# One transfer for both batches in the tail stores, and a last output piece halved between two engines

## The chip, the cores and the metric

The kernel runs on one core of a Trainium2 chip. The metric is the device time of one launch in microseconds. Before the change it was 333.6 us, the median of 3 runs (333.51 to 333.68).

## The reference

A sliding-window attention with ALiBi bias feeds a gated feed-forward block:

```python
B, H, S, D = 8, 8, 576, 64
scores = q @ k.transpose(0, 1, 3, 2) / np.sqrt(D) + slopes * -abs(rel)   # where 0 <= rel < 128
attn = softmax(scores)
x = (attn @ v).transpose(0, 2, 1, 3).reshape(B * S, H * D)               # 4608 x 512
g = x @ w_gate                                                           # 512 x 1536
out = (g * sigmoid(g) * (x @ w_val)) @ w_out                             # 4608 x 512, float32
```

## The kernel before, in words

The 4608 tokens are handled in 9 blocks of 512. Blocks 0 to 7 hold the first 512 tokens of one batch each. A batch has 576 tokens, so 64 are left over in each of the 8 batches; block 8, the tail block, collects these 8 times 64 tokens. Its four tiles of 128 rows hold one pair of batches each: rows 0 to 63 of tile `j` are the last 64 tokens of batch `2j`, rows 64 to 127 those of batch `2j + 1`. In the output in memory those two groups of 64 rows lie 576 rows apart.

The output product of a block is a seven-product scheme, the generator `strassen(n, t)`. For `t` = 0 and 1 it makes the tiles `t` (called `top`) and `t + 2` (called `low`), each 128 rows by 512 columns in float32. Each product is 6 matmuls into a 128x256 piece of PSUM (`X`, `Y` or `p2`); VectorE (`half_plus`, L605) or ScalarE (L612, L623, L626) takes the piece out, and `store` (L507) sends finished rows to memory. A `yield` stands after each product.

Block 8 is the last work of the kernel, and its output is written nowhere earlier. Its two generators are advanced in a fixed order; one step of generator 0 is done earlier, and then

```python
for t in (1, 0, 1, 0, 1, 0, 1, 0, 0, 1, 0, 1, 1):
    next(ends[t])
```

By this order the stores of block 8 are, in time: the left half of tile 1 (second product of generator 1), all of tile 0 (sixth product of generator 0), the right half of tile 3 (fifth of generator 1), all of tile 2 (seventh of generator 0), the right half of tile 1 (sixth of generator 1), and the left half of tile 3 (seventh of generator 1). The last piece, `low[:, 0:HC]` of generator 1 with HC = 256 columns, is taken from `X` by one VectorE instruction (L639).

Before the change a store of a tail tile is two issues of 64 rows, one for each batch. The first of these six stores puts both on SyncE's queue (SP); the other five put one on SP's queue and one on ScalarE's (ACT). Stores of blocks 0 to 7 are one issue of 128 rows on SP's queue. SP has no other work at the end, and ACT has no compute left after the piece `u2s` of generator 1.

Of the kernel before, what the change touches and what calls it, by code (L numbers as in the profile page):

```python
# [16 lines left out]
P = 128  # L17
# [39 lines left out]
def kernel(  # L57
# [10 lines left out]
    nc = tc.nc  # L68
    B, H, S, D = q.shape
    NTOK, DM = out.shape  # L70
# [3 lines left out]
    NSUP = B // 2  # L74
# [418 lines left out]
        val(n, m, wide(n, m, "v"), c0)  # L493
        yield

    def rows_of(n, j):
        if n == 8:
            return [(0, 64, 2 * j * S + 512), (64, 128, (2 * j + 1) * S + 512)]
        return [(0, 128, n * S + j * P)]

    held_stores = []
    queue_unit = [None]

    def store(n, j, osb, c0=0, c1=512, two=False):
        def now():
            for i, (p0, p1, r0) in enumerate(rows_of(n, j)):
                (nc.scalar if two and i else nc.sync).dma_start(out[r0:r0 + p1 - p0, c0:c1],  # L507
                                                                osb[p0:p1, c0:c1])
        if queue_unit[0] is None:
            now()  # L510
        else:
            held_stores.append((queue_unit[0], now))

    def project(n, j, pool, tag, bufs):
        po = pool.tile([P, DM], FP32, name="po", tag=tag, bufs=bufs)
        for m0 in range(0, NMB, 4):
            for i in range(m0, m0 + 4):
                m = NMB - 1 - i if n == 0 else i
                nc.tensor.matmul(po, hT[n][:, m, j * P:(j + 1) * P], wo_sb[:, m, :],  # L519
                                 start=(i == 0), stop=(i == NMB - 1))  # L520
            if m0 + 4 == NMB:
                osb = opool.tile([P, DM], FP32, name="osb", tag="osb")
                nc.scalar.mul(osb, po, 0.5)
                store(n, j, osb)
            yield
# [5 lines left out]
    HC = DM // 2  # L531
# [40 lines left out]
    def strassen(n, t):  # L572

        h = hT[n]
        A11, A12 = h[:, 0:HM, 0:256], h[:, HM:NMB, 0:256]
        S1, A22 = h[:, 0:HM, 256:512], h[:, HM:NMB, 256:512]
        S2, S3, S4 = hsum[n]
        cols = slice(t * P, (t + 1) * P)
        end = n == NBLK - 1
        seeded = SEVEN_FROM <= n + 1 < NBLK  # L580
        factor = 1.0 if n >= SEVEN_FROM else 0.5
        if end:
            X, Y = (ps_a.tile([P, HC], FP32, name="po", tag="a", bufs=4) for _ in range(2))
            p2 = ps_f.tile([P, HC], FP32, name="p2", tag="gv")
        else:
            po = ps_f.tile([P, 2, HC], FP32, name="po", tag="po", bufs=1)
            X, Y = po[:, 0, :], po[:, 1, :]
            p2 = (ps_f.tile([P, HC], FP32, name="p2", tag="gv") if seeded
                  else ps_a.tile([P, HC], FP32, name="p2", tag="a"))
        top, low = (opool.tile([P, DM], FP32, name="osb", tag="osb") for _ in range(2))  # L590
        if end and t:
            spare = [opool.tile([P, DM], FP32, name="osb", tag="osb") for _ in range(2)]
            p1s, p5s, u2s = spare[0][:, 0:HC], spare[0][:, HC:DM], spare[1][:, 0:HC]
        else:
            p1s, p5s, u2s = (supool.tile([P, HC], FP32, name=i, tag=i, bufs=1)
                             for i in ("p1s", "p5s", "u2s"))

        def product(dst, a, b, start=False):
            for m in range(HM):
                nc.tensor.matmul(dst, a[:, m, cols], b[:, m, :], start=(start and m == 0),  # L600
                                 stop=(m == HM - 1), skip_group_check=True)

        def half_plus(dst, a, b):
            with tc.high_priority() if n + 1 < SEVEN_FROM else ExitStack():
                nc.vector.scalar_tensor_tensor(out=dst, in0=a, scalar=factor, in1=b,  # L605
                                               op0=ALU.mult, op1=ALU.add)

        product(X, A11, B11, True)
        if seeded:
            nc.scalar.copy(p2, X)  # L610
        else:
            nc.scalar.mul(p1s, X, factor)  # L612
        yield
        product(p2, A12, B21, not seeded)
        if seeded:
            nc.vector.tensor_scalar_mul(top[:, 0:HC], p2, factor)
        else:
            half_plus(top[:, 0:HC], p2, p1s)
        if end and t:
            store(n, t, top, 0, HC)  # L620
        yield
        product(Y, S1, T1, end)
        nc.scalar.mul(p5s, Y, factor)  # L623
        yield
        product(X, S2, T2)
        nc.scalar.mul(u2s, X, factor)  # L626
        yield
        product(X, S3, T3)
        half_plus(low[:, HC:DM], X, p5s)
        if end and t:  # L630
            store(n, t + 2, low, HC, DM, True)
        yield
        product(Y, S4, B22)
        half_plus(top[:, HC:DM], Y, u2s)
        store(n, t, top, HC if end and t else 0, DM, end)
        yield
        product(X, A22, T4)
        if end:
            nc.vector.tensor_scalar_mul(low[:, 0:HC], X, factor)  # L639
        else:  # L640
            nc.scalar.mul(low[:, 0:HC], X, factor)
        store(n, t + 2, low, 0, HC if end and t else DM, end)
        yield


# [123 lines left out]
    def ffn():  # L769

        for n in range(NBLK):
            if n > 1:
                parts = chain(strassen(n - 1, 0), strassen(n - 1, 1))
# [38 lines left out]
            if n > 1:  # L812
                assert next(parts, 0) == 0
        ends = [strassen(NBLK - 1, t) for t in range(2)]
        tail = ExitStack()
        for n, k, name, which in seven_steps():
            if k == 0 and n > SEVEN_FROM:
                assert next(parts, 0) == 0
                parts = chain(strassen(n - 1, 0), strassen(n - 1, 1))
# [291 lines left out]
```

## Time and profile before

| What | Value |
|---|---|
| median of 3 runs | 333.6 us (333.51 to 333.68) |
| the profiled execution: time, span | 334.02 us, 332.2 us |
| TensorE busy | 323.4 us, 97% of the span |
| VectorE, ScalarE, GpSimd busy | 263.8, 224.3, 111.0 us |
| granted TensorE clock | 0.998 |
| stores from SP, 256 KB each | 32 issues, 2.4 us (median) from issue to landing |
| tail stores from SP | 5 of 64 KB and 2 of 128 KB, 2.3 and 2.5 us |
| tail stores from ACT | 3 of 64 KB and 2 of 128 KB, 2.6 us each |

The span runs from the first to the last instruction that the profile shows; the device time of the same execution is 1.8 us longer. "DMA share" in a table of windows is the mean busy share of the core's 16 DMA engines. A packet is one piece of memory that a DMA engine moves; for these stores it is one row, 2 KB for a whole tile and 1 KB for a half. A queue named q1 is SP's, q10 is ACT's.

### The profile page before, as it was taken

The page shows a single profiled execution, that of the slowest core. Times are in us where ns is not written, and L with a number is a line of the kernel's source. Part 1 is how long each engine was busy: PE and PEld are TensorE (multiplying, and loading weights), DVE is VectorE, ACT ScalarE, POOL GpSimd, SP SyncE. Part 2 cuts the span into 40 slices and gives each one's busy share as a digit, 9 for nine tenths or more (in the row PEclk, how much of TensorE's full clock was granted, in tenths as well). Part 3 has the DMA queues.
Part 4 walks back from the last instruction along what each step waited for, and adds up shares of the span by engine and source line. Part 5 has one row for each costly group of instructions (what it writes and reads, how often), then busy time and mean ns, then how long its engine had stood idle before and what let it go on. Part 6 is the DMA issues. An engine that isn't in the chain of part 4 may idle for free.

```text
span 332.2 us, 7692 instructions
## 1 busy us (share of the span) xinstructions
PE 323.4 (97%) x2911; PEld 216.1 (65%) x2911; DVE 263.8 (79%) x643; ACT 224.3 (68%) x446; POOL 111.0 (33%) x138
## 2 busy tenths in 40 slices
PE   8999999999999999999999999999999999999994
PEld 4665465444455656556556555566788888888884
DVE  4678878999796779877999799997754985775683
ACT  4886777464677868687777677774577666776650
POOL 8977776394963244537253100000000000000000
PEclk9999999999999999999999999999999999999999
DMA  9999999999999999999999991412100101001014
GB/s 152 174 180 176 175 186 166 121 145 173 143 179 170 137 185 143 170 142 155 173 161 174 135 180 32 83 32 79 65 32 35 63 2 63 32 36 64 2 63 129
DMA packets 167654, 39.09 MB, mean 118 GB/s; under 512 B 155456, under 2 KB 163264, under 8 KB 167616
## 3 DMA queue, kind: packets, MB, share of 16 engines
q0 software_dynamic: 118880, 18.62, 80.6%
q1 hardware_dynamic: 48048, 19.35, 33.8%
q10 hardware_dynamic: 688, 0.62, 0.6%
q8 instruction: 23, 0.38, 0.5%
q14 instruction: 15, 0.12, 0.1%
HBM read 37.91 MB, written 9.44 MB: 143 GB/s over the span
## 4 chain that ended last, share of the span: by engine, by line
PE 75%; DVE 16%; ACT 4%; issue 3%; DVEq 0%; ACTq 0%
PE po L600 16%; PE pg L452 13%; PE pv L452 13%; PE gX L689 10%; PE gY L689 5%; PE av L392 4%; DVE uu L471 4%; PE p L600 3%; PE ps L322 3%; PE gZ L689 2%; DVE ex L334 2%; DVE x L396 2%; ACT tt L470 1%; PE po L519 1%; ACT exc L364 1%
## 5 line engine op out<-in xcount | busy, mean ns | idle before, releaser
L452 PE MATMUL pv<-xT,wv_sb 128*128 128x512 f16 (+2 forms) x312 | 76.5, 363 | 0.5 <-DVE uu L471 0.4
L452 PE MATMUL pg<-xT,wg_sb 128*128 128x512 f16 (+2 forms) x324 | 76.6, 355 | 0.1
L470 ACT ACTIVATE tt<-pg 128x512 f16<-128x512 f32 x68 | 41.0, 605 | 32.7 <-PE pg L452 31.3
L328 ACT ACTIVATE ex<-ps 128x512 f16<-128x512 f32 x96 | 50.9, 610 | 4.9 <-PE ps L322 4.9
L471 DVE SCALAR_TENSOR_TENSOR uu<-tt,pg 128x512 f16<-128x512 f16 x67 | 45.6, 680 | 10.4 <-ACT tt L470 9.8
L194 POOL DMA_DIRECT2D kn<-in_k_dram x39 | 33.4, 861 | 47.7 <-DMA kT<-kn 40.7
L452 PEld LDWEIGHTS <-wg_sb 128*128 128x128 f16 x324 | 28.8, 98 | 24.5 <-issue 2.2
L452 PEld LDWEIGHTS <-wv_sb 128*128 128x128 f16 x312 | 27.9, 98 | 25.5 <-issue 2.8
L600 PEld LDWEIGHTS <-hT 128*128 128x128 f16 x384 | 37.2, 98 | 10.7 <-issue 0.8
L188 POOL DMA_DIRECT2D va<-in_v_dram x40 | 34.3, 861 | 15.0 <-DMA kn<-in_k_dram 4.0
L194 POOL DMA_DIRECT2D qn<-in_q_dram x39 | 33.4, 864 | 9.2 <-DMA va<-in_v_dram 5.7
L484 ACT CAST hT<-pv 128x512 f16<-128x512 f32 x44 | 26.3, 598 | 12.9 <-PE pv L452 12.9
L600 PEld LDWEIGHTS <-S 128*128 128x128 f16 x288 | 27.5, 98 | 8.2 <-issue 1.9
L334 DVE TENSOR_TENSOR ex<-ex,m_reg 128x1024 f16<-128x1024 f16 x42 | 28.6, 684 | 3.9 <-ACT ex L328 3.8
L396 DVE TENSOR_TENSOR x<-av,rec 128x256 f16<-128x256 f32 x72 | 28.5, 418 | 0.4
L600 PE MATMUL po<-T,S 128*128 128x256 f16 x192 | 25.9, 273 | 0.3 <-ACT u2s L626 0.3
L600 PE MATMUL po<-T,hT 128*128 128x256 f16 x192 | 26.0, 273 | 0.0
L364 ACT ACTIVATE exc<-psc 128x512 f16<-128x512 f32 x40 | 21.4, 608 | 1.4 <-PE psc L360 1.3
L743 DVE TENSOR_TENSOR hT<-s,v 128x512 f16<-128x512 f16 x18 | 7.6, 423 | 17.7 <-ACT s L742 17.7
L392 PEld LDWEIGHTS <-ex 128*128 128x128 f16 x384 | 17.6, 97 | 4.6 <-issue 1.5
L485 DVE TENSOR_TENSOR hT<-uu,hT 128x512 f16<-128x512 f16 x44 | 18.3, 417 | 2.0 <-ACT hT L484 1.0
L392 PE MATMUL av<-va,ex 128*128 128x65 f16 x384 | 19.4, 193 | 0.6 <-ACT ex L328 0.3
(131 smaller groups left out, 550.6 us busy)
## 6 DMA issues: line engine op xcount, KB each, us to landing
out_dram<-osb SPq DMA_DIRECT2D x32, 256.0 KB, 2.4
va<-in_v_dram POOLq DMA_DIRECT2D x32, 128.0 KB, 8.6
qn<-in_q_dram POOLq DMA_DIRECT2D x31, 128.0 KB, 8.3
kn<-in_k_dram POOLq DMA_DIRECT2D x31, 128.0 KB, 8.3
wg_sb<-in_moe_w_gate_dram POOLq DMA_DIRECT2D x6, 256.0 KB, 7.6
wo_sb<-in_moe_w_out_dram POOLq DMA_DIRECT2D x3, 512.0 KB, 8.2
wv_sb<-in_moe_w_val_dram POOLq DMA_DIRECT2D x5, 256.0 KB, 7.6
kn<-in_k_dram POOLq DMA_DIRECT2D x8, 64.0 KB, 10.3
```

What stands on the lines that cost most here:

```text
L188: nc.gpsimd.dma_start(va[rank][p0:p1, :, 0:D], src)
L194: nc.gpsimd.dma_start(t_[p0:p1], src)
L328: nc.scalar.activation(e[:, o:o + 2, :], banks[q4][par], AF.Exp, scale=scale)
L334: nc.vector.tensor_mul(e[:, o, :], e[:, o, :], reg[:, o, :])
L392: nc.tensor.matmul(av[:, j, :], w, val, start=(n == 0), stop=(n == len(todo) - 1))
L396: nc.vector.tensor_mul(x[:, 4 * half:4 * half + 4, :], av[:, :, 0:D], rec.broadcast_to([P, 4, D]))
L452: close.after = nc.tensor.matmul(ps[:, c0:c1], w[:, kb, ms], xT[n][:, kb, c0:c1], start=(kb == 0 and c0 == 0), stop=(kb == NKB - 1 and c1 ...
L470: nc.scalar.activation(tt, pg[:, c0:c1], AF.Tanh, scale=0.5)
L471: nc.vector.scalar_tensor_tensor(out=uu, in0=tt, scalar=one if (n, m) == PIN else 1.0, in1=pg[:, c0:c1], op0=ALU.add, op1=ALU.mult)
L484: nc.scalar.copy(h, pv)
L600: nc.tensor.matmul(dst, a[:, m, cols], b[:, m, :], start=(start and m == 0), stop=(m == HM - 1), skip_group_check=True)
L689: nc.tensor.matmul(dst[:, i, :], w[:, kb, c0 + i * P:c0 + (i + 1) * P], a[:, kb, :], start=(start and i == 0 and kb == 0), stop=(i == 1 an ...
```

## The change

A store of a tail tile becomes one issue: the output in memory is seen as (batch pair, batch of the pair, token, column), and the 128 rows of the tile go to a view of 2 x 64 rows. All of these go to SP's queue but one: the whole store of tile 2 goes to ACT's. The last piece, 128x256, is taken from PSUM by two instructions, columns 0 to 127 on VectorE and 128 to 255 on ScalarE. Stores of blocks 0 to 7 have the same rows, columns and queue as before.

```diff
-    def rows_of(n, j):
-        if n == 8:
-            return [(0, 64, 2 * j * S + 512), (64, 128, (2 * j + 1) * S + 512)]
-        return [(0, 128, n * S + j * P)]
...
+    tails_out = out.rearrange("(j n t) d -> j n t d", j=NSUP, n=2)
+
-    def store(n, j, osb, c0=0, c1=512, two=False):
+    def store(n, j, osb, c0=0, c1=512, by=None):
         def now():
-            for i, (p0, p1, r0) in enumerate(rows_of(n, j)):
-                (nc.scalar if two and i else nc.sync).dma_start(out[r0:r0 + p1 - p0, c0:c1],
-                                                                osb[p0:p1, c0:c1])
+            to = tails_out[j, :, 512:S, c0:c1] if n == 8 else out[n * S + j * P:n * S + (j + 1) * P, c0:c1]
+            (by or nc.sync).dma_start(to, osb[:, c0:c1])
...
         if end and t:
-            store(n, t + 2, low, HC, DM, True)
+            store(n, t + 2, low, HC, DM)
...
-        store(n, t, top, HC if end and t else 0, DM, end)
+        store(n, t, top, HC if end and t else 0, DM)
         yield
         product(X, A22, T4)
-        if end:
+        if end and t:
+            nc.vector.tensor_scalar_mul(low[:, 0:P], X[:, 0:P], factor)
+            nc.scalar.mul(low[:, P:HC], X[:, P:HC], factor)
+        elif end:
             nc.vector.tensor_scalar_mul(low[:, 0:HC], X, factor)
         else:
             nc.scalar.mul(low[:, 0:HC], X, factor)
-        store(n, t + 2, low, 0, HC if end and t else DM, end)
+        store(n, t + 2, low, 0, HC if end and t else DM, nc.scalar if end and not t else None)
```

## The prediction

> **What bounds the kernel now.** I read the page first: TensorE is busy for 97% of the span, so an edit that touches no matmul can only act before TensorE starts or after it ends. The edit touches the stores of the tail block alone, which all lie after 323 us. The chain of waits over the last 6 us says where TensorE lets go:
>
> ```profile
> span 332.2 us, 7692 instructions
> ...
> by line: PE po L600 24.8%; DVE osb L639 5.3%; issue 0.3%
> ...
> 325.98 1.98 PE po L600 x18
> 327.96 0.02 issue
> 327.98 0.42 DVE osb L639
> ```
>
> The last matmul ends at 327.96 and the last piece is out of PSUM at 328.40. The remaining 3.8 us belong to no engine. The windows table says who works there (the last two columns are DMA share and GB/s):
>
> ```profile
> 327.00:327.50 0.50, 0.50 (x7) 0.44 (x6) 0.20 (x2) 0.00 (x0) 0.00 (x0) 1.00 0.91 193
> 327.50:328.00 0.50, 0.44 (x5) 0.15 (x2) 0.34 (x2) 0.00 (x0) 0.00 (x0) 1.00 0.97 307
> ...
> 329.00:329.50 0.50, 0.00 (x0) 0.00 (x0) 0.00 (x0) 0.00 (x0) 0.00 (x0) 1.00 0.97 322
> ...
> 330.00:330.50 0.50, 0.00 (x0) 0.00 (x0) 0.00 (x0) 0.00 (x0) 0.00 (x0) 1.00 0.58 176
> 330.50:331.00 0.50, 0.00 (x0) 0.00 (x0) 0.00 (x0) 0.00 (x0) 0.00 (x0) 0.69 0.00 0
> ```
>
> From 327.0 to 330.4 all 16 DMA engines are near full. So the end is set by the DMA engines emptying the output: the last packets end at about 330.4, and 1.8 us later (completions, then the closing barrier) the span ends. Whatever slows these packets moves the end one for one. The tail stores are issued here (start, length, queue):
>
> ```profile
> 323.41 5.54 SPq L507 DMA_DIRECT2D out_dram<-osb  x7
> ...
> 325.89 3.37 ACTq L507 DMA_DIRECT2D out_dram<-osb  x5
> ...
> 328.44 0.52 SPq L507 DMA_DIRECT2D out_dram<-osb  x1
> ...
> 328.68 0.58 ACTq L507 DMA_DIRECT2D out_dram<-osb  x1
> ```
>
> The unit price of moving rows comes from three DMA views. First one 128-row, 256 KB store alone (318.3 to 320.3), then the whole of ACT's queue (300 to 334), then the first tail store, two times 64 rows of 1 KB (324 to 326):
>
> ```profile
> DMA packets 144, 0.26 MB, mean 131 GB/s; under 512 B 16, under 2 KB 16, under 8 KB 144
> ...
> q1 hardware_dynamic: 144, 0.26, 34.2%
> ```
> ```profile
> q10 hardware_dynamic: 400, 0.46, 4.0%
> ```
> ```profile
> q1 hardware_dynamic: 155, 0.13, 25.0%
> ```
>
> A 128-row store is 128 row packets and 16 tiny ones, so all 16 engines end a share of it. ACT's five 64-row stores make 5 x (64 + 16) = 400 packets: 16 shares again. Price of a 2 KB row: 34.2% x 16 engines x 2.0 us / 128 = 85 ns, 84 ns without the tiny packets. Price of a 1 KB row: 25.0% x 16 x 2.0 / 124 data packets recorded = 64 ns in the 64-row stores. In the last stretch (329.6 to 330.4, where the DMA view gives 46.3% and 34.3% for the two queues, 244 packets, 52 of them tiny) it is 51 ns; half of a 2 KB row would be 42 ns; the commonest single record is 46 ns, which I take.
>
> **The change part by part.**
>
> *Seven issues on SP become five, five on ACT become one.* A 128-row issue takes 0.33 us on SP (the store at 318.35), the 64-row ones 0.47 to 0.58 on SP and 0.56 to 0.78 on ACT. This removes about 2 us of queue time on SP and 2.5 on ACT, beside the transfers and not on the path, except that the last issue no longer stands at 328.68 behind ACT's earlier ones (0.3 us). Worth that much only if the DMA engines are idle then.
>
> *The shape of the transfer.* This is the step that decides. Every transfer in this trace has 64 or 128 as the outermost count on both sides and ends in 16 shares. The new view of memory begins with a count of 2, the batches, 576 rows apart, which can't be folded into the 64 rows; the SBUF side begins with 128. No row shows how such a pair is dealt out. Bounds: 16 shares by rows, as all stores now (8 rows for each engine), or shares by the outermost count that both sides have, that is 2 shares of 64 rows on 2 engines. I take the second: each share must be a whole piece of both patterns, and the only cut at the outermost level that 2 and 128 both allow is in two.
>
> Sum for 2 engines. Both get 64 rows of each of the six stores: four half tiles, 4 x 64 x 46 ns = 11.8 us, and two whole ones, 2 x 64 x 84 ns = 10.8 us; 22.6 us of packets for each engine, where now the same 1 MB is spread over 16. The first store is issued at 323.41; the first packet follows 0.83 us (the store at 318.35) to 1.2 us later, so at about 324.4. The first store alone holds its engines to 327.3, and the second is issued at 325.88, so the two engines never run dry. Last packet: 324.4 + 22.6 = 347.0. With the same 1.8 us behind it the span is 348.8, that is 16.6 us more than 332.2. The profiled execution (334.02, 1.8 beside its span) becomes 350.6; the runs' median lies 0.4 lower, so **350.2 us**.
>
> Bounds of that sum: 42 and 84 ns with the early start give 324.2 + 21.5 + 1.8 = 347.5, or 348.9 as a median. 64 ns and 110 ns (the latter is what is left for a 2 KB row in the crowded stretch from 326.9 to 330.5: 85.3% x 16 x 3.6 us = 49.1 us, less 385 rows at 51 ns and the tiny packets, over 256 rows) give 16.4 + 14.1 = 30.5 us from 324.6, a span of 356.9 and a median of 358.3.
>
> The Trainium skill weighs in on both sides here. Its page "DMA: Bandwidth & Descriptors", section "Why a DMA increments its semaphore by 16 and not by 1", states that the number of engines is the largest up to 16 that divides the slowest dimension of both patterns: 2 here, and the sum above; the trace's 16 shares for 64 and 128 rows agree with it but show no smaller count. The same page's "Rules for kernel authors" advises one 128-partition transfer in place of two for the two halves of the partitions, which is this change in so many words; taken alone it would give the 333.3 us of the first rival.
>
> *The last piece on two engines.* VectorE takes 424 ns for 128x256. ScalarE takes 384 for 256 columns and 598 for 512 (the pieces of L641 and L523), so 128 columns should cost it 384 - 107 = 277 ns, and VectorE between 212 (half) and 424. The piece is ready 0.0 to 0.15 us earlier. ACT's instruction stands behind ACT's issue of tile 2 (ready at 327.09, 0.56 to 0.78 long, so free at 327.9), just ahead of the last matmul at 327.96. With 2 engines none of it shows, since the last store queues behind some 16 us of packets. If that issue waits for room in a queue whose engines are behind, ACT's half is late with it, and the last store with that; no row shows such a wait. Bounds: nothing, or the last 2.9 us of packets begin only after all others are out, 0.8 to 1.2 us more.
>
> **The rivals.**
>
> *Dealt over 16 engines by rows, no change (not slower).* For it: every store of the trace has 16 shares. Against: none has an outermost count below 64. Then the DMA engines are the bound as now with the same rows. Tile 0 is one issue, with its first packet 0.83 us after 325.88, at 326.7 and not 327.0: up to 0.3 us less, 333.3 us. It decides if any cut by rows is made.
>
> *Dealt over 16 and the engines run freer.* If all rows then cost 84 and 46 ns, the packets after 325.88 are (256 x 84 + 384 x 46) / 16 = 2.4 us where they take 3.4 now. The last piece then limits: issued at 328.3, first packet 0.83 later, half a microsecond of packets, 329.6 and not 330.4. That is 0.8 to 1 us less, 332.7 us.
>
> *Two engines that slow each other or are held up,* at 64 and 110 ns, 358 us, and about 360 with the hold-up of the last issue. Against it: two engines take a small part of the bandwidth that 16 fill.
>
> **How the numbers follow.** Two engines: 0.88, of which 0.82 within 348.5 to 360 (packets at 46/84 up to the crowded price with the hold-up) and the rest outside. Sixteen engines without a gain: 0.06; with one: 0.06. I give the two engines most because it is the only cut that both patterns share and the trace's 16 shares never come without a multiple of 16 in front. The measurement tells 0.2%, that is 0.7 us, from no change; 333.3 counts as the same, 332.7 as faster. So faster 0.06, same 0.06, slower 0.88.
>
> **What would show it.** Right: the same 512 + 256 row packets of the tail block, but 12 tiny ones in place of 192; a DMA share near 0.125 (2 of 16) from 324.4 to about 347 at some 45 GB/s; stores that land 4 to 19 us after their issue; the last matmul still near 328. Wrong: a DMA share near 0.9 from 327 to 330 and 16 tiny packets for each store, which would be the rivals with 16 engines; or a share near 0.125 with rows at 64 ns and more, which would be my price per row.

## The result, and the profile after

The change makes the kernel slower: 350.16 us (median of 5 runs, 349.77 to 350.49) against 333.61 us before (5 runs, 333.51 to 333.73), a ratio of 1.0487 with a 95% interval of 1.0475 to 1.0498. The forecast was 350.2 us.

The page's first lines, and the chain of waits from 326 us on, in the changed kernel:

```profile
span 348.4 us, 7683 instructions
...
PE 323.3 (93%) x2911; PEld 216.0 (62%) x2911; DVE 263.9 (76%) x643; ACT 224.5 (64%) x447; POOL 111.0 (32%) x138
```
```profile
325.96 1.04 PE po L596 x10
327.00 1.23 DMA out_dram<-osb
328.23 0.04 issue
328.26 0.28 ACT osb L636
```

TensorE's busy time and its 2911 matmuls are those of before (323.4 us). In the chain, the stretch "DMA out_dram<-osb" covers ACT's issue of tile 2 (327.00 to 328.14), which stands ahead of ScalarE's half of the last piece. The last compute instruction ends at 328.54, where it was 328.40. The span is 16.2 us longer, and all but 0.1 us of it lies behind the last compute instruction. The windows (start and end, length, five engines, clock, DMA share, GB/s) show what fills it:

```profile
325.00:327.00 2.00, 2.00 (x21) 1.78 (x20) 1.33 (x4) 0.00 (x0) 0.00 (x0) 1.00 0.13 36
327.00:329.00 2.00, 0.81 (x8) 0.49 (x5) 0.72 (x2) 0.28 (x1) 0.00 (x0) 1.00 0.13 38
...
332.00:336.00 4.00, 0.00 (x0) 0.00 (x0) 0.00 (x0) 0.00 (x0) 0.00 (x0) 0.50 0.13 51
336.00:340.00 4.00, 0.00 (x0) 0.00 (x0) 0.00 (x0) 0.00 (x0) 0.00 (x0) 0.50 0.13 50
...
346.00:347.00 1.00, 0.00 (x0) 0.00 (x0) 0.00 (x0) 0.00 (x0) 0.00 (x0) 0.50 0.12 44
347.00:349.00 2.00, 0.00 (x0) 0.00 (x0) 0.00 (x0) 0.00 (x0) 0.00 (x0) 0.50 0.00 0
```

A DMA share of 0.13 is 2 of 16 engines, from the first tail store to 347. Before, the share was 0.85 to 0.97 for three microseconds. The rate is about 50 GB/s, where it was about 300. The DMA view of the changed kernel from 324 to 349 (packets, then the two queues with packets, MB and share of 16 engines):

```profile
DMA packets 782, 1.07 MB, mean 43 GB/s; under 512 B 12, under 2 KB 524, under 8 KB 780
...
q1 hardware_dynamic: 650, 0.79, 9.2%
q10 hardware_dynamic: 130, 0.26, 2.7%
```

The same 768 row packets (512 of 1 KB, 256 of 2 KB) leave, but 12 tiny packets stand beside them: two for each of the six stores, where each of the twelve issues before had 16. Each tail store ran on two engines. The packets took (9.2% + 2.7%) x 16 x 25 us = 47.6 us, 23.8 us for each of the two.

### The profile page after: what moved, and what is told of

It is laid out like the page before. It is cut to its first block, busy times and chain, and to the rows that moved or that the text cites. A ratio compares the mean times of both kernels' runs of the same rounds, so it can differ in the third digit from the quotient of the medians.

```text
span 348.4 us, 7683 instructions
## 1 busy us (share of the span) xinstructions
PE 323.3 (93%) x2911; PEld 216.0 (62%) x2911; DVE 263.9 (76%) x643; ACT 224.5 (64%) x447; POOL 111.0 (32%) x138
## 4 chain that ended last, share of the span: by engine, by line
PE 73%; DVE 14%; ACT 4%; issue 2%; DMA 0%; DVEq 0%; ACTq 0%
PE po L596 16%; PE pg L452 13%; PE pv L452 13%; PE gX L688 9%; PE gY L688 5%; PE av L392 4%; DVE uu L471 3%; PE ps L322 3%; PE p L596 3%; PE gZ L688 2%; DVE x L396 1%; PE po L515 1%; DVE ex L334 1%; ACT exc L364 1%; ACT tt L470 1%
```

## The experiments

The theory: the outermost counts of the two sides of a transfer set the number of DMA engines; 2 and 128 allow two, and the end moves by the time in which two engines empty the tail. The rivals: one issue over two far places is slow by itself; the halved piece or the move of a store to ACT's queue costs part of it. All ratios are to the kernel before, on the same chip.

**The counts turned round.** One edit to the changed kernel, so that the outermost count of the memory side is 64:

```diff
-            to = tails_out[j, :, 512:S, c0:c1] if n == 8 else ...
+            to = tails_out[j, :, 512:S, c0:c1].rearrange("n t d -> t n d") if n == 8 else ...
```

> The six tail stores keep their issues, queues and bytes, but the view of memory is turned to 64 x 2 rows, so that its outermost count is 64 instead of 2. The rows of each tail tile land in another order (row p goes to batch p mod 2, token p div 2); nothing else differs. Theory (the common outermost count sets the number of engines): 16 engines, 16 tiny packets for each store, DMA share near 0.9 from 327 to 330, and 332.7 to 333.4 us. Rival (one issue over two places 576 rows apart is slow by itself, whatever the order of its counts): still about 350 us with a DMA share of 0.13.

Measured: 333.47 us, ratio 0.9988 (0.9979 to 0.9997). Its DMA view from 324 to 349, and its window from 327.5 to 328.0:

```profile
DMA packets 866, 1.07 MB, mean 43 GB/s; under 512 B 96, under 2 KB 608, under 8 KB 864
```
```profile
327.50:328.00 0.50, 0.50 (x5) 0.24 (x3) 0.42 (x1) 0.00 (x0) 0.00 (x0) 1.00 0.98 365
```

The issues, queues, places in memory and bytes are the same; only the order in which the two counts are named differs, and with it which row of a tile lands where. There are 96 tiny packets, 16 for each store, the share reaches 0.98, and the 16.5 us are gone (the time is 0.1 us above the expected range). One issue over two places is not slow by itself.

**Other counts.** Eight and four pieces instead of two, so that the count changes, and with it the places of the rows in memory:

```diff
-    tails_out = out.rearrange("(j n t) d -> j n t d", j=NSUP, n=2)
+    tails_out = out.rearrange("(n t) d -> n t d", n=8)
...
-            to = tails_out[j, :, 512:S, c0:c1] if n == 8 else ...
+            to = tails_out[:, 512 + 16 * j:528 + 16 * j, c0:c1] if n == 8 else ...
```

> The view of memory is 8 batches x 16 tokens instead of 2 x 64: each store of a tail tile writes 16 of the tail tokens of every batch, so the tail rows land permuted. Issues, queues and bytes are as in the changed kernel. Theory: 8 engines with 16 rows each of every store. After the first store they are busy from about 326.6 for 16 x (2 x 84 + 3 x 46 ns) = 4.9 us, to 331.5; with 1.4 to 1.8 us behind it a span of 333.1 and about 334.9 us. Rival: about 350 us.

```diff
-    tails_out = out.rearrange("(j n t) d -> j n t d", j=NSUP, n=2)
+    tails_out = out.rearrange("(j n t) d -> j n t d", j=2, n=4)
...
-            to = tails_out[j, :, 512:S, c0:c1] if n == 8 else ...
+            to = tails_out[j // 2, :, 512 + 32 * (j % 2):544 + 32 * (j % 2), c0:c1] if n == 8 else ...
```

> The view of memory is 4 batches x 32 tokens: each store of a tail tile writes half of the tail tokens of four batches, so the tail rows land permuted. Issues, queues and bytes as in the changed kernel. Theory (common outermost count = engines): 4 engines with 32 rows each. From 327.0 on (the first packet of tile 0 with 8 engines) 32 x (2 x 84 + 3 x 46 ns) = 9.8 us, to 336.8, and 1.4 us behind it: a span of 338.2 and 340.0 us; if the rows start as slowly as they did on 8 engines, up to 1.9 us more. 8 tiny packets more than on 2 engines in the first store's window: 4 for each store. Rival (only a count of 2 is bad): 335 us or less.

Measured: 336.81 us with eight (1.0087, 1.0073 to 1.0100) and 342.78 us with four (1.0267, 1.0252 to 1.0281). The lines of tiny packets of the two runs, eight first, both from 324 to 349:

```profile
DMA packets 818, 1.07 MB, mean 43 GB/s; under 512 B 48, under 2 KB 560, under 8 KB 816
```
```profile
DMA packets 794, 1.07 MB, mean 43 GB/s; under 512 B 24, under 2 KB 536, under 8 KB 792
```

48 / 6 = 8 and 24 / 6 = 4 tiny packets for each store, and the DMA share was 0.52 with eight pieces (328.5 to 332) and 0.26 with four (329 to 334): the number of engines is the outermost count. The packet time for each engine is the sum of the two queues' shares, times 16 x 25 us, over the engines; beside it the sum at 84 and 46 ns a row:

| Outermost count | Tiny packets per store | Packet time of one engine | At 84 and 46 ns | Last packet ends | Time |
|---|---|---|---|---|---|
| 2 (the change) | 2 | 23.8 us | 22.5 us | 346.97 us | 350.16 us |
| 4 | 4 | 14.4 us | 11.3 us | 339.46 us | 342.78 us |
| 8 | 8 | 7.1 us | 5.6 us | 333.48 us | 336.81 us |
| 64 | 16 | 3.0 us | 2.8 us | 330.43 us | 333.47 us |

The engine counts came as expected, the times did not: with 4 pieces 0.9 us above the upper end of the forecast (340.0 to 341.9), with 8 pieces 1.9 us above 334.9. Both runs show single 2 KB rows that took several hundred ns, in 4 pieces one of 1.07 us; in 8 pieces 28 of the 34 rows over 150 ns start between 327.0 and 328.7. Two stretches of the run with 8 pieces:

```profile
327.00:328.50 1.50, 0.81 (x8) 0.48 (x5) 0.72 (x2) 0.15 (x1) 0.00 (x0) 1.00 0.48 78
328.50:332.00 3.50, 0.00 (x0) 0.00 (x0) 0.00 (x0) 0.13 (x1) 0.00 (x0) 0.69 0.52 178
```

At nearly the same share of busy engines (0.48 and 0.52) the first stretch moves 78 GB/s and the second 178. One run asked whether the distance in memory does this. Its edit is shown against the run with 8 pieces:

```diff
-            to = tails_out[:, 512 + 16 * j:528 + 16 * j, c0:c1] if n == 8 else ...
+            to = out[1024 * j:1024 * j + 520, c0:c1].rearrange("(n t) d -> n t d", n=8)[:, 0:16] if n == 8 else ...
```

> As the run with 8 batches x 16 tokens, but the eight pieces of 16 rows lie 65 rows apart in memory instead of 576 (the tail rows overwrite rows of other blocks and their own are left unwritten). Engines, rows per engine, SBUF side, issues and bytes are the same. It asks why rows of 2 KB took 139 ns on SP's queue there. Theory (it comes from the places in memory, 1.18 MB apart): rows at 84 to 90 ns, last packet near 331.7, 334.9 us. Rival (it comes from the SBUF side or from 8 engines as such): 336.8 us as before.

Measured: 336.38 us (1.0072, 1.0057 to 1.0087), 2 KB rows on SP's queue at a mean of 137 ns after 139. It isn't the distance: 65 rows apart are as slow as 576. What is left is the SBUF side (the tile that a store reads) or the number of engines as such. If each engine takes 16 consecutive rows, the eight begin in partitions 16 apart. The Trainium skill ("DMA: Bandwidth & Descriptors", section "The descriptor swizzle") says which partitions share a port; by its list partitions 0 and 32 do, so shares that start 16 or 32 rows apart would meet in pairs, and shares 64 apart would not. That would fit slow rows with 4 and 8 pieces and few with 2. Slow rows stand with 16 engines too, where an issue takes 64 partitions alone: 2 KB rows took 131 ns on average on SP's queue and 93 on ACT's in the kernel before, 139 and 136 in the run with two issues below, and 86 in the 64 x 2 run, whose issues take all 128. But no run here changed the partitions alone, so it stays open.

**Undoing the one transfer alone.** The changed kernel with its queues and its halved piece, but two issues of 64 rows again:

```diff
-            (by or nc.sync).dma_start(to, osb[:, c0:c1])
+            if n == 8:
+                for i in range(2):
+                    (by or nc.sync).dma_start(to[i], osb[64 * i:64 * i + 64, c0:c1])
+            else:
+                nc.sync.dma_start(to, osb[:, c0:c1])
```

> The changed kernel with only its one transfer over both batches undone: each tail store is again two issues of 64 rows, both on the queue that the change chose (SP, and ACT for tile 2); the halved last piece stays. Theory: 16 engines again; SP now makes ten issues of about 0.5 us, eight of them after 325.8, so the last ends at about 329.9 and its packets at 330.9: 334.0 to 334.4 us. Rival (the halved piece or the move of tile 2 to ACT cost part of the 16.5 us): over 336 us.

Measured: 334.88 us, 1.0032 (1.0019 to 1.0045), half a microsecond above the expectation. Its DMA view from 324 to 349 has 192 tiny packets, 16 for each of twelve issues, and the timeline of SP's queue from 329 to 331 says where the half microsecond comes from:

```profile
DMA packets 962, 1.07 MB, mean 43 GB/s; under 512 B 192, under 2 KB 704, under 8 KB 960
```
```profile
328.87 1.87 SPq L506 DMA_DIRECT2D out_dram<-osb  x3
```

Three issues take 1.87 us, so an issue costs about 0.6 and not 0.5, and the last ends at 330.7. So with ten issues on it SP's queue sets the end; the next run, with the issues spread over both queues as before, is 0.8 us shorter. The change without its one transfer comes to 1.1 us (0.6 to 1.5 by the interval), and that belongs to the ten issues, which the changed kernel does not make: with its queues, its halves and the 64 x 2 order the time was 333.47.

**The halved piece alone,** in the kernel before, and **the whole piece** in the changed kernel:

```diff
-        if end:
+        if end and t:
+            nc.vector.tensor_scalar_mul(low[:, 0:P], X[:, 0:P], factor)
+            nc.scalar.mul(low[:, P:HC], X[:, P:HC], factor)
+        elif end:
             nc.vector.tensor_scalar_mul(low[:, 0:HC], X, factor)
```

> The kernel before with the last piece halved between VectorE and ScalarE; the stores stay two issues of 64 rows. Theory: ScalarE's half now stands behind two issues of ACT (to 328.6), so it is ready at about 328.9 where the whole piece was at 328.4, and the last store goes out 0.2 to 0.4 us later, partly under the DMA engines' backlog: 333.6 to 334.0 us. Rival (the piece's readiness was the bound and halving helps): 333.4 us.

> The changed kernel with the last piece taken whole by VectorE (L639 of the kernel before); the six stores stay one issue each to 2 x 64 rows. Theory (the two engines' queue of rows covers the piece): 350.2 us, within 0.4. Rival (the halves or ACT's part in them cost time): 349.5 us or less.

Measured: 334.07 us for the first (1.0007, 0.9997 to 1.0018): not told apart from no change, with ScalarE's half at 329.02 behind ACT's issues, as expected. For the second 350.20 us (1.0484, 1.0461 to 1.0506): the piece does not matter under two engines. Why it doesn't help under 16 engines either, the chain of waits in the run with 64 x 2 rows shows, where ACT's queue is free in time:

```profile
325.97 2.09 PE po L596 x19
328.06 0.02 issue
328.08 0.30 DVE osb L635
328.38 0.02 issue
328.40 0.28 ACT osb L636
```

ScalarE's half waits for VectorE's half; the instruction that waits names VectorE's semaphore. Both read one PSUM tile and write one tile `low`; which of the two makes the framework that places the waits order them, no run shows. The halves take 0.60 us one after the other, where the whole piece takes 0.42. Taking the piece whole there:

> The 64 x 2 view (tail rows land permuted, 16 engines) with the last piece taken by VectorE alone. In the 64 x 2 run with halves ScalarE's half waited for VectorE's half, 0.29 + 0.03 + 0.28 = 0.60 us for the piece against 0.42 whole. Theory (the halves run one after the other and that lies on the path): the last issue leaves 0.18 us earlier, 333.3 us where the same chip had 333.47. Rival (the DMA engines' backlog hides it): 333.5 us.

Measured: 333.60 us, 0.9990 (0.9981 to 0.9999), beside 0.9988 for the halves. A difference of 0.1 us can't be told apart here; that the halves run in turn is shown, that it costs time is not.

**One narrow store, early or late.** In the kernel before, one of the six stores made one issue to 2 x 64 rows, `(3, 0)` for the last and `(1, 0)` for the first:

```diff
+    tails_out = out.rearrange("(j n t) d -> j n t d", j=NSUP, n=2)
...
+            if n == 8 and (j, c0) == (3, 0):
+                nc.sync.dma_start(tails_out[j, :, 512:S, c0:c1], osb[:, c0:c1])
+                return
             for i, (p0, p1, r0) in enumerate(rows_of(n, j)):
```

> The kernel before, with the last store alone (left half of tile 3, 128 KB) made one issue to the view of 2 x 64 rows; the other five stores stay two issues of 64 rows. Theory: two engines get 64 rows of 1 KB each, 64 x 46 to 51 ns = 2.9 to 3.3 us, behind their share of the other stores, which ends at about 330.1: last packet at 333.0 to 333.4 where it was 330.4, less 0.3 us that the completions of fewer engines save: 336.1 us (335.7 to 336.7). Rival (one narrow store is hidden by the others, only six in a row cost): within 0.5 us of 333.7.

> The kernel before, with the first tail store alone (left half of tile 1, 128 KB) made one issue to the view of 2 x 64 rows. Theory: its two engines are busy from 324.5 to 327.4, when all others wait until 327.0 anyway; two engines start the rest 0.4 us late and the end moves by 0 to 0.4 us: 333.7 to 334.1 us. Rival (a narrow store costs the same wherever it stands, 2.7 us as the last one did): 336.4 us.

Measured: 336.37 us with the last (1.0077, 1.0062 to 1.0092) and 334.38 with the first (1.0010, 1.0001 to 1.0020), beside 333.70 and 333.94 on their chips. Two windows of the run with the last store narrow:

```profile
327.00:329.50 2.50, 0.68 (x7) 0.37 (x4) 0.85 (x2) 0.00 (x0) 0.00 (x0) 1.00 0.93 282
330.50:332.50 2.00, 0.00 (x0) 0.00 (x0) 0.00 (x0) 0.00 (x0) 0.00 (x0) 0.50 0.13 40
```

Fourteen engines are done before 330 and two work on to 332.9. The same 128 KB cost 2.7 us at the end and 0.4 us (0.0 to 0.7 by the interval) at the beginning, where the engines had nothing else to do.

**A version with the right rows on 16 engines.** The query rows of the tail tiles are loaded in turn from the two batches (partition 2t + n is token t of batch n), the masks of the tail unit follow, each store is one issue to the 64 x 2 view, and the last piece stays whole:

```diff
...
-        to, of = ((msk[0][:, :, 0:64], reg[:, :, 128:192]),
+        to, of = ((by_batch[0][:, :, :, 0], reg[:, :, 128:192]),     # and so for the other three
...
-                nc.gpsimd.dma_start(t_[p0:p1], src)
+                nc.gpsimd.dma_start(t_[p0 // 64:P:2] if name == "q" and rank % 9 == 8 else t_[p0:p1], src)
...
```

> The version that the runs point to, with the right rows: the tail tiles' query rows are loaded interleaved (row p is batch p mod 2, token p div 2), the three masks of the tail unit follow, each tail store is one issue to the 64 x 2 view, the last piece stays whole on VectorE. Expected as the run with permuted rows, 333.3 us, up to 0.3 us more if the strided zeroing and copying of masks shows at the start; ahead of the kernel before by 0.1 to 0.5 us. Rival (it pays nothing over two issues on two queues): 333.7 us.

Measured: 333.33 us beside 333.70, ratio 0.9982 (0.9972 to 0.9992). It is faster than both kernels, 0.4 us faster than the one before. Two of its windows:

```profile
328.50:329.00 0.50, 0.00 (x0) 0.00 (x0) 0.17 (x1) 0.00 (x0) 0.00 (x0) 1.00 0.59 219
...
329.80:329.95 0.15, 0.00 (x0) 0.00 (x0) 0.00 (x0) 0.00 (x0) 0.00 (x0) 1.00 0.19 55
```

The DMA engines now have room between the stores, and what limits is the last piece (out of PSUM at 328.67), its issue (at 328.74) and its first packet (at 329.97). In the profiles the gain lies in two places: from the last matmul to the last packet 2.3 us pass where it was 2.5, and behind the last packet 1.45 us where it was 1.81. Every run with six single issues has 1.41 to 1.45 us there, and those with 11 or 12 issues have 1.58 to 1.81; why, no run shows.

## Why the prediction was right, point by point

- **Two engines** (the step that decides): shown by the 12 tiny packets, the share of 0.13, and the four counts of the table. The prediction reached it by reasoning on the two patterns, for the trace before held no such transfer. The Trainium skill's rule ("DMA: Bandwidth & Descriptors", section "Why a DMA increments its semaphore by 16 and not by 1") agrees in all of these: 2, 4, 8 and 16 engines measured for outermost counts of 2, 4, 8 and 64 beside 128. The advice of one 128-partition transfer in that page's "Rules for kernel authors" holds in the 64 x 2 order and costs 16.5 us in the 2 x 64 order.
- **The sum.** First packet forecast at 324.4, measured 324.58, 1.3 us after its issue where 0.83 to 1.2 were taken; last packet 347.0, measured 346.97. The rows were priced at 46 and 84 ns; the commonest records are these, and with some slow ones the engine's packet time was 23.8 us for the 22.6 forecast, part of it overlapped, since 22.4 us lie between first and last packet. Behind the last packet the forecast had 1.8 us, as before; it was 1.4. So the span came out as 348.4 for 348.8. That the time is met to 0.1 us is luck: the forecast also took 0.4 us off, because the profiled execution before lay that much above the median, and here the two are alike (350.18 and 350.16). The two errors of 0.4 us cancel.
- **SP's and ACT's issues.** Six issues for twelve, as said, but each of the first three took 0.51 to 0.69 us and not 0.33, without weight in the sum. The hold-up that the prediction bounded at 0.8 to 1.2 us did appear, in the queues alone. The timeline of SP's queue from 327 to 334, then from 334 to 339:

```profile
327.72 11.10 SPq L504 DMA_DIRECT2D out_dram<-osb  x2
```
```profile
333.23 5.59 SPq L504 DMA_DIRECT2D out_dram<-osb  x1
```

  The last two issues took 5.41 and 5.59 us, with engines far behind. The last ended at 338.8, well before the engines came to its rows (its two tiny packets are at 346.9, 64 rows of 46 ns after about 344), so it cost nothing.
- **The halved piece: this step was wrong,** without weight in the sum. It was to be ready 0.0 to 0.15 us earlier. The durations were right (292 and 277 ns for the 277 and 212 to 424 forecast), but the two halves don't run side by side, and ACT's issue of tile 2 took 1.14 us where 0.56 to 0.78 was taken. In the changed kernel that issue and VectorE's half both end at 328.14, and ScalarE's half starts at 328.26; the piece was ready at 328.54, 0.69 us after VectorE began it, where the whole piece had taken 0.42. The prediction looked at what stands ahead on ACT's queue, and not at who else touches the same tiles.
- **The rivals.** The first (16 engines, no change, 333.3) is what the 64 x 2 run gave, 333.47; the second (packets at 84 and 46 ns on 16 engines) had the price of the rows right, 3.0 us of packets for each engine, but not the time of 332.7: the last piece's issue came at 328.71 and not 328.3, and its first packet 1.2 us later and not 0.83; 1.7 us passed from the issue to the last packet. The third (two engines that slow each other or are held up, 358 to 360 us) did not come: nearly all rows stayed at 46 and 84 ns, and the hold-up cost nothing.

## What to carry to other kernels

Before folding two stores into one, look at the outermost count of both sides of the new pattern: here 2, 4 and 8 beside 128 gave that many engines and 64 gave all 16, so the same 128 rows named in the other order (64 x 2, not 2 x 64) ran eight times as wide. Count the tiny packets per transfer and read the DMA share: 0.13 is two engines. And a narrow store cost 2.7 us as the last one and 0.4 us as the first, so the last store is the one to look at first.

## What the runs showed of the hardware that was not expected

- With two engines behind, SP's last two issues took 5.41 and 5.59 us; with sixteen they took 0.54. Lateness alone does not do it: with four engines, whose last packet ended at 339.46, SP made four issues within 3.36 us (its timeline from 325 to 330 below). How many rows may wait before an issue is held, no run shows. ACT's issue of tile 2 took 1.14 us with two engines, 1.15 and 1.23 with four and eight, and 0.66 with sixteen.

```profile
325.62 3.36 SPq L504 DMA_DIRECT2D out_dram<-osb  x4
```

- On SP's queue in the tail, an issue of 64 x 2 rows took 0.54 to 0.67 us, one of 2 x 64 rows 0.51 to 0.69 where it wasn't held, and one of 64 plain rows 0.47 to 0.59. The 0.33 us of a plain 128-row issue is that of the stretch from 233 to 318 us in the kernel before; ahead of it such issues took 0.38 to 0.67, one 1.83. What makes a tail issue dearer than 0.33, no run shows.
- Nearly equal shares of busy engines (0.48 and 0.52) moved 78 and 178 GB/s in one run (8 pieces), and bringing the pieces closer in memory didn't mend it.
